# Block-sparse attention with a mixture of experts: gathered v rows interleaved by slot, edge blocks joined with a running maximum, masks made later

## The chip, the cores and the metric

One core of a Trainium2 chip runs the program. The metric is the device time of one execution in microseconds (us), as a median of several runs. The engines are PE (matrix products; its weight loads are listed as PEld), DVE (vector), ACT (scalar and table functions), POOL (general, and the issuer of gathers by index) and SP (issuer of most DMA transfers). PSUM is the memory that PE writes to, SBUF the one that it reads from.

## The reference

There are 4 batches of 8 heads, 768 positions and head dimension 64. Positions form 24 blocks of 32. A query block sees its own block and both neighbours, the first and the last block, and three blocks that the input `sampled_blocks` names for it; the first and the last query block see everything.

```python
scores = scale * np.matmul(q, k.transpose(0, 1, 3, 2))
mask = np.abs(blk_i - blk_j) <= window
mask = mask | (blk_i == 0) | (blk_j == 0) | (blk_i == n_blocks - 1) | (blk_j == n_blocks - 1)
for qb in range(n_blocks):
    for kb in sampled_blocks[qb]:
        mask[qb * block:(qb + 1) * block, kb * block:(kb + 1) * block] = True
scores = np.where(mask, scores, -1000000000.0)
attn = np.exp(scores - np.max(scores, axis=-1, keepdims=True))
attn = attn / (np.sum(attn, axis=-1, keepdims=True) + 1e-09)
attn_out = np.matmul(attn, v)
...
for e in range(E):
    h = np.maximum(x @ w1[e], 0.0)
    out += p[:, e:e + 1] * (h @ w2[e])
```

`x` is the attention output with a token's 512 numbers in a row, 3072 tokens in all. There are 4 experts with 1024 hidden numbers.

## The kernel before

The order of all instructions on all engines is the order of the program's text. Attention works in units, 16 a batch. Each unit has four steps: S (scores, maximum, exponential), T (PE transposes the probabilities), A (the product with v) and X (PE transposes the result into `xr`, the input of the experts).

The first four units of a batch are of the class `Edge`. They treat the first and the last query block (`i` = 0, 1) against all keys, in two halves of 384 keys (`m` = 0, 1). The maximum of each half is kept in `mx`, its sum in `sums`, and the product of the first half in `eo`. A of the second half joins both: it forms the common maximum `top`, the two weights `ew` (DVE, then an exponential on ACT, then DVE again), and the weighted and normalised sum `xe`, which X transposes into `xt`.

The other twelve are of the class `Group`. A unit treats four query blocks and half of the heads. A query row has 8 slots of 32 keys: the window's three blocks, the first block, three sampled blocks, the last block. In S, PE writes scores of two heads into each of two PSUM tiles `s`; DVE adds the mask `mk` and takes the maximum in one instruction (L321, whose result goes to the SBUF tile `p`), and ACT takes the exponential in place (L324). In T, four transposes of 128 columns go into `tp`, and ACT or DVE copies them to `pt`. So after the transpose the partition of a key is its slot in a half of four, times 32, plus its row in the block. v must lie in SBUF in that same order: `v[:, i, 0]` has the window and the first block, `v[:, i, 1]` the sampled blocks and the last one.

`load_v0` (batch 0) and `load_v` (later) bring v: one SP transfer for the window's 96 rows of two query blocks, one for the first block's 32, and a gather by POOL for each query block with the row numbers `vidx`. In batch 0 six tiles are used in turn; the last block's rows are put there once for each, by SP, and the gathers bring 96 rows. The row numbers come from `row_numbers`: two small matmuls, `rows` and `floor`, turn the sampled block numbers into rows. `spread_mask` makes the mask of all groups: a reduction and a product on DVE, a matmul `mps` and a copy to `mask`. `sampled_block` reads a block number into a register of ACT or POOL, and `copy_k` copies the sampled key blocks into `kr` with it. Both `rows`, `floor`, `mps` and the transposes `tw` and `tp` of batch 0 take turns in the PSUM pool `a`, which has two buffers.

Batch 0's attention runs alone, about 100 us. Its loop takes n from 0 to 18 and issues S of unit n, X of n - 3, A of n - 2 and T of n - 1, with loads and weight preparation between. Then the experts of batch b - 1 run with the attention of batch b between their pieces; `drive` interleaves them by planned times. There the transposes share the two PSUM buffers of `s`, and ACT copies both halves of T. The experts' additions on DVE (L810, L843, L942 and others) empty PSUM tiles that PE then fills again; L698 and L932 are the experts' matmuls.

Of the kernel before, what the change touches and what calls it, by code (L numbers as in the profile page):

```python
# [8 lines left out]
F32 = mybir.dt.float32  # L9
# [14 lines left out]
def attention_moe_kernel(ctx: ExitStack, tc, qb, kb, vr, sampled, sampled_t, probs, w1, w2, out):  # L24
# [122 lines left out]
    def load_v0(t, c):  # L147

        js = blocks(t)[c:c + 2]
        if not js:  # L150
            return
        turn = vturn[0]
        vturn[0] += 1
        if turn < 6:
            vtiles.append(pool["v"].tile([P, 2, 2, DM], F32, name=f"v{turn}"))
        v = vtiles[turn % 6]
        rows = vr[(js[0] - 1) * BLOCK:(js[0] + 2) * BLOCK]
        nc.sync.dma_start(v[:3 * BLOCK, :len(js), 0],
                          bass.AP(rows.tensor, rows.offset,
                                  [[DM, 3 * BLOCK], [BLOCK * DM, len(js)], [1, DM]]))  # L160
        if turn < 6:
            nc.sync.dma_start(v[3 * BLOCK:, :, 0],
                              vr[:BLOCK].unsqueeze(1).broadcast_to([BLOCK, 2, DM]))
            nc.sync.dma_start(v[3 * BLOCK:, :, 1],
                              vr[S - BLOCK:S].unsqueeze(1).broadcast_to([BLOCK, 2, DM]))
        for i, j in enumerate(js):
            nc.gpsimd.indirect_dma_start(
                out=v[:3 * BLOCK, i, 1], out_offset=None, in_=vr, element_offset=0,
                in_offset=bass.IndirectOffsetOnAxis(ap=vidx[:3 * BLOCK, j:j + 1], axis=0))
            gathered[0, t][2][c + i] = v[:, i]  # L170

    def load_v(b, t, cs=range(QG)):
        js = blocks(t)
        for c in range(min(cs), min(max(cs) + 1, len(js)), 2):
            n = min(2, len(js) - c)
            v = pool["v"].tile([P, 2, 2, DM], F32, name="v")
            rows = vr[b * S + (js[c] - 1) * BLOCK:b * S + (js[c] + 2) * BLOCK]
            nc.sync.dma_start(v[:3 * BLOCK, :n, 0],
                              bass.AP(rows.tensor, rows.offset,
                                      [[DM, 3 * BLOCK], [BLOCK * DM, n], [1, DM]]))  # L180
            nc.sync.dma_start(v[3 * BLOCK:, :n, 0],
                              vr[b * S:b * S + BLOCK].unsqueeze(1).broadcast_to([BLOCK, n, DM]))
            for i in range(n):
                nc.gpsimd.indirect_dma_start(  # L184
                    out=v[:, i, 1], out_offset=None, in_=vr, element_offset=b * S * DM,
                    in_offset=bass.IndirectOffsetOnAxis(ap=vidx[:, js[c + i]:js[c + i] + 1], axis=0))
                gathered[b, t][2][c + i] = v[:, i]

# [13 lines left out]
    for c in range(QG):  # L202
        sampled_block(1 + c, 1)
# [3 lines left out]
    nc.gpsimd.affine_select(out=lead, in_=lead, pattern=[[1, P]], compare_op=ALU.is_ge,  # L207
                            fill=0.0, base=0, channel_multiplier=-BLOCK)
    nc.gpsimd.affine_select(out=lead, in_=lead, pattern=[[-1, P]], compare_op=ALU.is_ge,
                            fill=0.0, base=BLOCK - 1, channel_multiplier=BLOCK)  # L210
# [29 lines left out]
    def row_numbers():  # L240
# [7 lines left out]
        nc.vector.tensor_sub(within, within, floor_[:, :1])  # L248
# [18 lines left out]

    def spread_mask():
        ind4 = p1.tile([NB, P], F32, name="ind4")
        nc.vector.reduce_sum(ind4, ind.rearrange("n t p -> n p t"), axis=AX.X)  # L270
        nc.vector.tensor_mul(sel, sel, bad.unsqueeze(1).broadcast_to([NB, NG, SLOTS]))
        mps = pool["a"].tile([P, NG, SLOTS], F32, name="mps", tag="a")
        nc.tensor.matmul(mps.rearrange("p t n -> p (t n)"), ind4, sel.rearrange("p t n -> p (t n)"),
                         start=True, stop=True)
        nc.vector.tensor_copy(mask, mps)
# [13 lines left out]
    class Group:  # L289
# [4 lines left out]
        def S(self):  # L294
# [21 lines left out]
            for i in range(HH):  # L316
                for h in range(2):
                    m = 2 * i + h
                    mx = at.tile([P, 1], F32, name="mx", bufs=4)
                    p = self.p[:n, m]  # L320
                    nc.vector.tensor_tensor_reduce(p.rearrange("p (a b) -> p a b", b=BLOCK),  # L321
                                                   s[h][:n, i], mk, -SCALE, 3.0e38, ALU.add, ALU.min,
                                                   mx[:n])
                    nc.scalar.activation(p, p, AF.Exp, bias=mx[:n], scale=-1.0,  # L324
                                         accum_out=self.sums[:n, m:m + 1])
# [43 lines left out]
    class Edge:  # L369
# [4 lines left out]
        def S(self):  # L374
# [10 lines left out]
            if m == 0:  # L385
                edge["S"] = [at.tile([P, 2, 2], F32, name=f"edge{j}") for j in range(2)]
            self.mx, self.sums = edge["S"]
            self.p = pool["p"].tile([P, S], F32, name="pw", tag="p")
            nm = at.tile([P, 2], F32, name="nm2")
            for h in range(2):  # L390
                nc.vector.reduce_max(self.mx[:, m, h:h + 1], s[h], axis=AX.X)
            nc.vector.tensor_scalar(nm, self.mx[:, m], -SCALE, None, op0=ALU.mult)
            for h in range(2):
                nc.scalar.activation(self.p[:, h * HS:(h + 1) * HS], s[h], AF.Exp, bias=nm[:, h:h + 1],
                                     scale=SCALE, accum_out=self.sums[:, m, h:h + 1])

# [9 lines left out]
        def A(self):  # L406
# [10 lines left out]
            if self.m == 0:  # L417
# [3 lines left out]
            top = at.tile([P, 2], F32, name="top")  # L421
            nc.vector.tensor_max(top, self.mx[:, 0], self.mx[:, 1])
            w = at.tile([P, 2, 2], F32, name="ew")
            nc.vector.tensor_sub(w, self.mx, top.unsqueeze(1).broadcast_to([P, 2, 2]))
            nc.scalar.activation(w, w, AF.Exp, scale=SCALE)
            nc.vector.tensor_mul(self.sums, self.sums, w)
            rec = at.tile([P, 2], F32, name="rec2")
            nc.vector.scalar_tensor_tensor(rec, self.sums[:, 0], 1e-9, self.sums[:, 1],
                                           op0=ALU.add, op1=ALU.add)
            nc.vector.reciprocal(rec, rec)  # L430
            nc.vector.tensor_mul(w, w, rec.unsqueeze(1).broadcast_to([P, 2, 2]))
            self.xg = at.tile([P, P], F32, name="xe", bufs=1)
            xe = self.xg.rearrange("p (h d) -> p h d", d=D)
            eo = edge["o"]
            nc.vector.tensor_mul(xe, eo, w[:, 0].unsqueeze(2).broadcast_to([P, 2, D]))
            nc.vector.tensor_mul(eo, o, w[:, 1].unsqueeze(2).broadcast_to([P, 2, D]))
            nc.vector.tensor_add(xe, xe, eo)
# [648 lines left out]
    with ExitStack() as only:  # L1086
# [11 lines left out]
        rows = {0: (0, 2), 1: (1, 0), 2: (1, 2), 5: (2, 0), 6: (2, 2)}  # L1098
        rows.update({2 * t + 1: (t, 0) for t in range(3, NG)})
        rows.update({2 * t + 2: (t, 2) for t in range(3, NG)})  # L1100
# [4 lines left out]
        for n in range(N + 3):  # L1105
            if n < N:
                us[n].S()
            if n == 0:
                row_numbers()
                load_v0(0, 0)  # L1110
            if n == 1:
                spread_mask()
                copy_k(0, 0)
# [7 lines left out]
            if n in rows:  # L1121
                t, c = rows[n]
                if c == 0:
# [12 lines left out]
            if n < 4:  # L1136
                for c in range(QG + 5 * n, min(QG + 5 * n + 5, NB - 2)):
# [127 lines left out]
```

## Time and profile before

| | us |
|---|---|
| median of 3 runs | 1277.0 |
| lowest and highest | 1276.53, 1279.74 |
| the profiled execution, whole | 1275.48 |
| its span, from the first to the last instruction | 1273.5 |
| PE busy | 1207.7 |
| DVE busy | 847.6 |
| POOL busy | 840.4 |
| ACT busy | 520.3 |

The mean granted clock of PE is 0.983 of full speed. The span is what the trace covers; the 2.0 us around it are start and end. A view's row has a start or a count, a duration, the engine, the line of the kernel (L321 is line 321), the operation with output and input, and in brackets the idle time of that engine just before, with what ended it. Busy time of an engine that nobody waits for costs nothing; what counts is idle time of PE, which is nearly full, and what it waits for.

### The profile page before, as it was taken

The numbers are of one execution on the slowest core, as the hardware profiler recorded it, in microseconds if no ns is written. First come the engines' busy times: TensorE is split into PE (matmuls) and PEld (weight loads), VectorE is DVE, ScalarE is ACT, GpSimd is POOL, SyncE is SP. The second block draws the span as 40 slices with busy tenths as digits, with TensorE's granted clock in tenths as the row PEclk, the third lists the DMA queues.
The fourth block names the chain that finished last, engine by engine and source line by source line (L and its number), as shares of the span: only waits on it lengthen the run. The fifth ranks groups of instructions, "written<-read, shape, count | busy, mean of one in ns | idle before, by whom it ended". The sixth has DMA issues, their size and how long they took to land.

```text
span 1273.5 us, 32610 instructions
## 1 busy us (share of the span) xinstructions
PE 1207.7 (95%) x12583; PEld 1111.6 (87%) x12583; DVE 847.6 (67%) x1710; ACT 520.3 (41%) x1259; POOL 840.4 (66%) x788
## 2 busy tenths in 40 slices
PE   6778899999999899999999989999999999999997
PEld 3667778888888888999999978998999999999997
DVE  5565577676765566766676875766676776666667
ACT  3473545656454244444442343444443323222221
POOL 6353778888867475765746774676754777666663
PEclk8899999999999999999999999999999999999999
DMA  9675588989877866899868875998886777887774
GB/s 290 168 238 177 184 321 276 346 290 341 312 286 290 302 215 210 271 271 294 263 218 302 257 253 170 286 269 254 272 261 215 235 250 251 260 267 248 250 243 149
DMA packets 212822, 326.52 MB, mean 256 GB/s; under 512 B 15995, under 2 KB 115932, under 8 KB 212668
## 3 DMA queue, kind: packets, MB, share of 16 engines
q1 hardware_dynamic: 205936, 302.80, 73.8%
q0 software_dynamic: 6688, 21.63, 5.6%
q8 instruction: 100, 1.64, 0.5%
q14 instruction: 54, 0.44, 0.1%
q10 hardware_dynamic: 44, 0.00, 0.0%
HBM read 256.69 MB, written 67.68 MB: 255 GB/s over the span
## 4 chain that ended last, share of the span: by engine, by line
PE 63%; DVE 4%; DMA 3%; issue 1%; ACT 1%; POOL 0%; SPq 0%; DVEq 0%; ACTq 0%
PE w L698 16%; PE u L932 15%; PE v L698 12%; PE v L932 11%; PE o L346 2%; PE tp L333 2%; DMA wo<-kept 2%; PE po L768 1%; PE s L311 1%; PE s L306 1%; DVE ha L810 1%; DVE tot L942 1%; DMA v<-in_vr_dram,vidx 1%; DVE xo L475 0%; DMA k<-in_kb_dram 0%
## 5 line engine op out<-in xcount | busy, mean ns | idle before, releaser
L856 POOL TENSOR_TENSOR ho<-ha,ho 128x768 fp32r<-128x768 f32 x165 | 324.2, 1974 | 233.4 <-ACT ho L855 219.4
L698 PE MATMUL w<-xo,wo 128*128 128x384 f32 x1536 | 315.6, 342 | 18.8 <-DVE ha L843 11.4
L698 PEld LDWEIGHTS w<-xo,wo 128*128 128x128 f32 x1536 | 271.6, 190 | 30.6 <-DVE ha L843 14.0
L698 PE MATMUL v<-xo,wo 128*128 128x384 f32 x1200 | 244.9, 340 | 5.4 <-DVE hl L717 1.5
L855 ACT CAST ho<-ha 128x768 fp32r<-128x768 f32 x168 | 139.5, 836 | 266.9 <-DVE ha L810 95.6
L932 PE MATMUL u<-ho,w2o 128*128 128x384 f32 x1128 | 229.5, 339 | 0.4 <-issue 0.4
L698 PEld LDWEIGHTS v<-xo,wo 128*128 128x128 f32 x1200 | 212.5, 189 | 12.5 <-DVE hl L717 2.1
L932 PEld LDWEIGHTS u<-ho,w2o 128*128 128x128 f32 x1128 | 198.9, 189 | 2.6 <-issue 2.0
L932 PE MATMUL v<-ho,w2o 128*128 128x384 f32 x888 | 181.2, 341 | 2.5 <-issue 1.5
L932 PEld LDWEIGHTS v<-ho,w2o 128*128 128x128 f32 x888 | 156.6, 190 | 4.7 <-issue 2.2
L942 DVE TENSOR_TENSOR tot<-v,tot 128x384 f32<-128x384 f32 x184 | 97.7, 550 | 62.6 <-PE v L932 60.2
L942 DVE TENSOR_TENSOR tot<-u,tot 128x384 f32<-128x384 f32 x180 | 99.0, 553 | 54.1 <-PE u L932 52.4
L324 ACT ACTIVATE p<-p,mx 128x256 f32<-128x256 f32 (+1 forms) x192 | 95.4, 498 | 89.5 <-DVE mx L321 89.3
L810 DVE SCALAR_TENSOR_TENSOR ha<-ha,pb 128x384 f32<-128x384 f32 x126 | 127.4, 1011 | 4.4
L768 PE MATMUL po<-w2o,hh 128*128 128x512 f32 x384 | 123.2, 402 | 5.3 <-DVE oacc L783 3.5
L588 POOL TENSOR_TENSOR wo<-r,wo 128x256 fp32r<-128x256 f32 x92 | 73.9, 810 | 44.7 <-ACT wo L587 44.6
L321 DVE CUSTOM_DVE_ANT_1 p<-s,mask 128x256 f32<-128x256 f32 (+1 forms) x192 | 69.7, 417 | 29.0 <-PE s L311 28.7
L184 POOL DMA_INDIRECT v<-in_vr_dram,vidx x66 | 65.3, 989 | 29.9 <-issue 13.5
L768 PEld LDWEIGHTS po<-w2o,hh 128*128 128x128 f32 x384 | 68.7, 188 | 15.5 <-DVE oacc L783 4.8
L768 PE MATMUL po<-w2o,hl 128*128 128x512 f32 x192 | 75.7, 394 | 0.0
L346 PEld LDWEIGHTS o<-v,pt 128*32 128x32 f32 x2816 | 47.8, 112 | 18.7 <-issue 14.9
L346 PE MATMUL o<-v,pt 128*32 128x64 f32 x2816 | 57.5, 225 | 5.5 <-issue 4.2
(162 smaller groups left out, 1642.5 us busy)
## 6 DMA issues: line engine op xcount, KB each, us to landing
w2o<-kept SPq DMA_DIRECT2D x168, 512.0 KB
wo<-kept SPq DMA_DIRECT2D x318, 256.0 KB
kept<-wo SPq DMA_DIRECT2D x106, 256.0 KB
v<-in_vr_dram SPq DMA_DIRECT2D x44, 384.0 KB
kept<-w2o SPq DMA_DIRECT2D x32, 512.0 KB
r<-in_w_dram SPq DMA_DIRECT2D x16, 512.0 KB
r<-in_w_dram SPq DMA_DIRECT2D x32, 256.0 KB
kept<-t SPq DMA_DIRECT2D x32, 256.0 KB
```

The lines of the kernel that those rows point to most:

```text
L184: nc.gpsimd.indirect_dma_start(out=v[:, i, 1], out_offset=None, in_=vr, element_offset=b * S * DM, in_offset=bass.IndirectOffsetOnAxis(ap= ...
L321: nc.vector.tensor_tensor_reduce(p.rearrange("p (a b) -> p a b", b=BLOCK), s[h][:n, i], mk, -SCALE, 3.0e38, ALU.add, ALU.min, mx[:n])
L324: nc.scalar.activation(p, p, AF.Exp, bias=mx[:n], scale=-1.0, accum_out=self.sums[:n, m:m + 1])
L346: nc.tensor.matmul(o[cs, m], self.pt[:, 2 * m + k, cs], vs[c][:, k, e], start=k == 0, stop=k == 1)
L588: nc.gpsimd.tensor_sub(o[:, 1], src, f32(o[:, 0]))
L698: nc.tensor.matmul(ps, w[:, wi, t], x[:, xi, t], start=fresh and m == 0, stop=m == 3 * KH - 1, skip_group_check=not fresh)
L768: nc.tensor.matmul(p, a[:, js], w[:, i], start=f == 0 and n == 0, stop=f == FT - 1 and n == 2)
L810: nc.vector.scalar_tensor_tensor(block(g, half), src, 0.0, q, op0=ALU.max, op1=ALU.mult)
L855: nc.scalar.copy(o[:, 0], src)
L856: eng.tensor_sub(o[:, 1], src, f32(o[:, 0]))
L932: nc.tensor.matmul(ps, w[:, j, wi, ds], h[:, hi, j], start=fresh and m == 0, stop=m == 5, skip_group_check=not fresh)
L942: nc.vector.tensor_add(t, ps, t)
```

## The change

Four things are changed.

1. v lies in SBUF with a key's partition at 4 x row + slot. The window's load becomes three SP transfers of 32 rows, each to every fourth partition; the first block's goes to every fourth one from 3. All gathers bring 128 rows, in batch 0 too, where the six separate transfers of the last block go. The matrix `lead` and the arithmetic behind `vidx` follow.
2. The probabilities take the same order: DVE writes the masked scores back into the PSUM tile `s`, and ACT reads them there and writes the exponentials to `p` in steps of four elements.
3. In an `Edge` unit the second half takes its maximum over both halves in S, and the weight of the first half is made there, with an exponential on ACT behind the scores' own. A scales the first half's sum and product by it, adds, and normalises.
4. In batch 0, `row_numbers` and the DVE part of `spread_mask` move from units 0 and 1 behind T of unit 0, the mask's matmul and `copy_k` behind T of unit 1. ACT reads eight block numbers ahead of the loop instead of four.

```diff
+    def window(v, b, js):
+        for m in range(3):
+            rows = vr[b * S + (js[0] + m - 1) * BLOCK:]
+            nc.sync.dma_start(v[m:P:QG, :len(js), 0],
+                              bass.AP(rows.tensor, rows.offset,
+                                      [[DM, BLOCK], [BLOCK * DM, len(js)], [1, DM]]))
+
+    def first_rows(v, b, n):
+        nc.sync.dma_start(v[3:P:QG, :n, 0],
+                          vr[b * S:b * S + BLOCK].unsqueeze(1).broadcast_to([BLOCK, n, DM]))
+
+    def gather(v, b, i, j):
+        nc.gpsimd.indirect_dma_start(
+            out=v[:, i, 1], out_offset=None, in_=vr, element_offset=b * S * DM,
+            in_offset=bass.IndirectOffsetOnAxis(ap=vidx[:, j:j + 1], axis=0))
...
-    for c in range(QG):
+    for c in range(2 * QG):
         sampled_block(1 + c, 1)
...
-        nc.vector.tensor_sub(within, within, floor_[:, :1])
+        nc.vector.scalar_tensor_tensor(within, floor_[:, :1], -1.0 / BLOCK, within,
+                                       op0=ALU.mult, op1=ALU.add)
+        nc.vector.tensor_scalar(within, within, 1.0 / QG, None, op0=ALU.mult)
...
-                    p = self.p[:n, m]
-                    nc.vector.tensor_tensor_reduce(p.rearrange("p (a b) -> p a b", b=BLOCK),
-                                                   s[h][:n, i], mk, -SCALE, 3.0e38, ALU.add, ALU.min,
-                                                   mx[:n])
-                    nc.scalar.activation(p, p, AF.Exp, bias=mx[:n], scale=-1.0,
-                                         accum_out=self.sums[:n, m:m + 1])
+                    p = self.p[:n, m].rearrange("p (a r b) -> p a b r", a=2, b=QG)
+                    sc = s[h][:n, i]
+                    nc.vector.tensor_tensor_reduce(sc, sc, mk, -SCALE, 3.0e38, ALU.add, ALU.min, mx[:n])
+                    nc.scalar.activation(p, sc.rearrange("p (a b) r -> p a b r", b=QG), AF.Exp,
+                                         bias=mx[:n], scale=-1.0, accum_out=self.sums[:n, m:m + 1])
...
+            if m == 1:
+                nc.vector.tensor_max(self.mx[:, 1], self.mx[:, 0], self.mx[:, 1])
             nc.vector.tensor_scalar(nm, self.mx[:, m], -SCALE, None, op0=ALU.mult)
+            if m == 1:
+                nc.vector.tensor_sub(self.w, self.mx[:, 0], self.mx[:, 1])
...
+            if m == 1:
+                nc.scalar.activation(self.w, self.w, AF.Exp, scale=SCALE)
...
-            if n == 0:
-                row_numbers()
-                load_v0(0, 0)
-            if n == 1:
-                spread_mask()
-                copy_k(0, 0)
...
+            if n == 1:
+                row_numbers()
+                spread_mask()
+            if n == 2:
+                place_mask()
+                copy_k(0, 0)
```

The order of the instructions shows three places. The first is the start of PE's program before, and then after; `sw` are scores of an Edge unit, `tw` its transposes, `ow` its products with v.

```order
L198 MATMUL idle<-zero 128x384 x4
L382 MATMUL sw<-k,qe 32x384 x8
L245 MATMUL rows<-slot,lead 128x24
L247 MATMUL floor<-quad,lead 128x128
L382 MATMUL sw<-k,qe 32x384 x8
L273 MATMUL mps<-sel,ind_312 128x48
L403 MATMUL tw<-ident,pw 128x128 x6
L382 MATMUL sw<-k,qe 32x384 x8
L415 MATMUL ow<-vn,ptw 32x64 x24
```

Here is the same place in the changed kernel.

```order
L199 MATMUL idle<-zero 128x384 x4
L387 MATMUL sw<-k,qe 32x384 x16
L416 MATMUL tw<-ident,pw 128x128 x6
L246 MATMUL rows<-slot,lead 128x24
L248 MATMUL floor<-quad,lead 128x128
L387 MATMUL sw<-k,qe 32x384 x8
L428 MATMUL ow<-vn,ptw 32x64 x24
L416 MATMUL tw<-ident,pw 128x128 x6
L279 MATMUL mps<-sel,ind_225 128x48
```

The scores of two units and the transposes of the first now come ahead of `rows`, and `mps` stands behind the second unit's transposes. The second place is DVE's program at the first join, before, with the semaphores that each row waits for:

```order
30 L391 TENSOR_REDUCE edge_484<-sw 128x1 [waits PE_49] x2
31 L392 TENSOR_SCALAR nm_593<-edge_484 128x2 [waits DVE_49,Activation_49]
32 L422 TENSOR_TENSOR top<-edge_221 128x2
33 L424 TENSOR_TENSOR ew<-edge_221,top 128x4 [waits DVE_49]
34 L426 TENSOR_TENSOR edge_222<-edge_222,ew 128x4 [waits Activation_49]
35 L428 SCALAR_TENSOR_TENSOR rec_630<-edge_222 128x2 [waits DVE_49]
36 L430 RECIPROCAL rec_630<-rec_630 128x2 [waits DVE_49]
37 L431 TENSOR_TENSOR ew<-ew,rec_630 128x4 [waits DVE_49]
38 L435 TENSOR_TENSOR xe<-eo,ew 128x128 [waits DVE_49]
39 L436 TENSOR_TENSOR eo<-ow,ew 128x128 [waits DVE_49,PE_49]
40 L437 TENSOR_TENSOR xe<-xe,eo 128x128 [waits DVE_49]
```

and after:

```order
33 L398 TENSOR_REDUCE edge_379<-sw 128x1 [waits PE_49] x2
34 L400 TENSOR_TENSOR edge_379<-edge_379 128x2 [waits DVE_49]
35 L401 TENSOR_SCALAR nm_587<-edge_379 128x2 [waits DVE_49,Activation_49]
36 L403 TENSOR_TENSOR ew<-edge_379 128x2
37 L435 TENSOR_TENSOR rec_621<-edge_259,ew 128x2 [waits Activation_49]
38 L436 SCALAR_TENSOR_TENSOR rec_621<-rec_621,edge_259 128x2 [waits DVE_49]
39 L437 RECIPROCAL rec_621<-rec_621 128x2 [waits DVE_49]
40 L440 SCALAR_TENSOR_TENSOR eo<-eo,ew,ow 128x64 [waits PE_49]
41 L440 SCALAR_TENSOR_TENSOR eo<-eo,ew,ow 128x64
42 L443 TENSOR_TENSOR xe<-eo,rec_621 128x128 [waits DVE_49]
```

The maximum and the weight stand with the scores, and the join waits for ACT on its first row alone, for a result that a row of an earlier step asked for. The third place is DVE's program in a Group unit (the second one of the batch, whose four reductions are of two PSUM tiles in turn), after:

```order
55 L328 ISA s,mx<-s,mask 128x256 [waits PE_49]
56 L328 ISA mx 128x1
57 L328 ISA s,mx<-s,mask 128x256 [waits PE_49]
58 L328 ISA mx 128x1
59 L328 ISA s,mx<-s,mask 128x256 [waits Activation_49]
60 L328 ISA mx 128x1
61 L328 ISA s,mx<-s,mask 128x256 [waits Activation_49]
62 L328 ISA mx 128x1
```

The third and the fourth wait for ACT, which is the first and the second exponential of the same unit. Before, they were `p,mx<-s,mask`, and what waits for ACT they had was for exponentials of the unit ahead.

More of the change, by code (lines that the diff above doesn't have):

```diff
@@ L176, in load_v @@
             v = pool["v"].tile([P, 2, 2, DM], F32, name="v")
[L177 to L182, printed above, removed]
+            window(v, b, js[c:c + n])
+            first_rows(v, b, n)
             for i in range(n):
-                nc.gpsimd.indirect_dma_start(
-                    out=v[:, i, 1], out_offset=None, in_=vr, element_offset=b * S * DM,
-                    in_offset=bass.IndirectOffsetOnAxis(ap=vidx[:, js[c + i]:js[c + i] + 1], axis=0))
+                gather(v, b, i, js[c + i])
                 gathered[b, t][2][c + i] = v[:, i]
@@ L386, in S @@
                 edge["S"] = [at.tile([P, 2, 2], F32, name=f"edge{j}") for j in range(2)]
+                edge["w"] = at.tile([P, 2], F32, name="ew")
             self.mx, self.sums = edge["S"]
+            self.w = edge["w"]
             self.p = pool["p"].tile([P, S], F32, name="pw", tag="p")
@@ L420, in A @@
                 return
[L421 to L426, printed above, removed]
             rec = at.tile([P, 2], F32, name="rec2")
-            nc.vector.scalar_tensor_tensor(rec, self.sums[:, 0], 1e-9, self.sums[:, 1],
-                                           op0=ALU.add, op1=ALU.add)
+            nc.vector.tensor_mul(rec, self.sums[:, 0], self.w)
+            nc.vector.scalar_tensor_tensor(rec, rec, 1e-9, self.sums[:, 1], op0=ALU.add, op1=ALU.add)
             nc.vector.reciprocal(rec, rec)
-            nc.vector.tensor_mul(w, w, rec.unsqueeze(1).broadcast_to([P, 2, 2]))
+            eo = edge["o"]
+            for h in range(2):
+                nc.vector.scalar_tensor_tensor(eo[:, h], eo[:, h], self.w[:, h:h + 1], o[:, h],
+                                               op0=ALU.mult, op1=ALU.add)
             self.xg = at.tile([P, P], F32, name="xe", bufs=1)
[L433 to L437, printed above, removed]
+            nc.vector.tensor_mul(self.xg.rearrange("p (h d) -> p h d", d=D), eo,
+                                 rec.unsqueeze(2).broadcast_to([P, 2, D]))
         def X(self):
@@ L1120, in attention_moe_kernel @@
                 us[n - 1].T(1)
-            if n in rows:
-                t, c = rows[n]
-                if c == 0:
+            if n == 1:
[4 more added lines that the diff above has]
+                copy_k(0, 0)
+            for t, c in rows.get(n, ()):
+                if c == 0 and t:
                     load_q(0, t)
@@ L1135, in attention_moe_kernel @@
                 taken += 1
-            if n < 4:
-                for c in range(QG + 5 * n, min(QG + 5 * n + 5, NB - 2)):
+            if 0 < n < 4:
+                for c in range(5 * n + 3, min(5 * n + 8, NB - 2)):
                     sampled_block(1 + c, 1)
```

31 lines of the change are left out of this document (12 added, 19 removed).

## The prediction

> **What bounds the kernel now.** I read the page first, for the engine that is full and for the one group of matmuls that still waits.
>
> ```profile
> span 1273.5 us, 32610 instructions
> PE 1207.7 (95%) x12583; PEld 1111.6 (87%) x12583; DVE 847.6 (67%) x1710; ACT 520.3 (41%) x1259; POOL 840.4 (66%) x788
> ...
> L698 PE MATMUL w<-xo,wo 128*128 128x384 f32 x1536 | 315.6, 342 | 18.8 <-DVE ha L843 11.4
> ```
>
> PE is busy for 95% of the span, so only its 65.8 idle us are to be had. The table by stage says where they lie.
>
> ```profile
> 0.00:31.00 31.00, 19.34 (x306) 0.87 0.97 287
> 41.00:100.00 59.00, 46.18 (x1271) 0.90 0.68 207
> 100.00:1273.00 1173.00, 1134.34 (x10759) 0.99 0.80 258
> ```
>
> Columns: length, PE busy, granted clock, DMA share, GB/s. PE idles 11.7 us in the first 31, 12.8 in the rest of batch 0's attention from 41 on, and 38.7 in the 1173 us behind. Two of PE's waits before 100 us that name no other engine matter below:
>
> ```profile
> PE s L306 <- issue: 6.1, 9, 2.6
> PE ow L415 <- issue: 2.8, 3, 1.2
> ```
>
> Columns: total, times, longest. "issue" is time for which the profile shows no wait. The waits that the change touches stand in PE's timeline (start, length, what it is, idle time before):
>
> ```profile
> 8.68 0.37 PE L245 MATMUL rows<-slot,lead 4*128 4x24 f32 x2 [1.53 <-DVE slot L243]
> 13.56 0.63 PE L273 MATMUL mps<-sel,ind 24*128 24x48 f32 x2 [3.40 <-DVE sel L271]
> 14.12 1.54 PE L403 MATMUL tw<-ident,pw 128*128 128x128 f32 x6
> 15.59 0.89 PE L382 MATMUL sw<-k,qe 64*32 64x384 f32 x8
> 19.65 0.88 PE L382 MATMUL sw<-k,qe 64*32 64x384 f32 x16
> 25.57 0.40 PE L306 MATMUL s<-k,q 64*32 64x96 f32 x16
> 29.23 0.33 PE L442 MATMUL xt<-ident,xe 128*128 128x128 f32 x1 [2.44 <-DVE xe L435]
> 35.59 0.40 PE L306 MATMUL s<-k,q 64*32 64x96 f32 x16
> 39.15 0.33 PE L442 MATMUL xt<-ident,xe 128*128 128x128 f32 x1 [2.16 <-DMA v<-in_vr_dram]
> ```
>
> The four idle times are rows, mps and, twice, xt. I call the units 0, 1, 2 ... in their order: S(0) is the first scores, T the transposes, A the product with v.
>
> **The start, step by step.** The mask leaves the path at 13.56, and two things take its place: ACT reads eight block numbers instead of four ahead of its first exponential, and the rows matmul stands behind T(0), in a PSUM buffer that ACT's copy of T(0) must have emptied.
>
> ```profile
> L123 ACTq TENSOR_LOAD <-sbrow x22: 275/278/478, 5.4 to 28.0; - x22
> L123 ACTq FUSED_REGOPS  x22: 147/147/167, 6.0 to 28.4; - x22
> ```
> ```profile
> 8.56 0.58 ACT L394 ACTIVATE pw<-sw,nm 128x384 f32<-128x384 f32 x1 [4.96 <-DVE slot L243]
> 15.06 0.48 ACT L404 COPY ptw<-tw 128x384 f32<-128x384 f32 x1 [1.00 <-issue]
> ...
> 36.91 0.19 ACT L425 ACTIVATE ew<-ew 128x4 f32<-128x4 f32 x1
> ```
> ```profile
> 10.73 1.02 DVE L391 TENSOR_REDUCE edge<-sw 128x1 f32<-128x384 f32 x2 [0.90 <-PE sw L382]
> ...
> 11.86 1.44 DVE L270 TENSOR_REDUCE ind<-ind 24x128 f32<-24x768 f32 x1
> ```
>
> The durations are the middle ones. A block number costs 0.278 + 0.147 us and the gaps around them, by my estimate 0.57 in all; from 5.4, eight end at about 10.0. Two exponentials take 1.2: those of S(0) then run 10.0 to 11.2, those of S(1) to 12.4, the new weight (0.2) to 12.6, the copy (0.48) to 13.1. T(0) itself can start at 11.2 instead of 14.12. rows (0.37) and the floor matmul behind it run from 13.1, and S(2) at about 13.7, 1.9 earlier than 15.59. A(0) and T(1) keep that. On DVE the row numbers come at 14.0, then the reduction (1.44), the maxima of S(2) (1.02 for two) and their scaling, and ACT's two exponentials and copy of T(1): 14.0 + 1.6 + 1.2 + 1.2 + 0.5 = 18.5 (0.2 for each small operation). The mask matmul waits for that copy, since it takes the buffer, so S(3) starts at 18.9, not 19.65: of 1.9 us, **0.75** is left. A(1), T(2) and S(4) follow with that.
>
> The first xt then waited 2.44 us for the join. In the new order the weight is ready with the scores, and behind A(1) there are two joining operations and one scaling left, some 1.1 us, while T(2) and S(4) take longer on PE. I count all **2.4**. So 3.2 us by 29.23, if POOL keeps up:
>
> ```profile
> 10.12 1.10 POOL L167 DMA_INDIRECT v<-in_vr_dram,vidx  x1 [4.15 <-DVE vidx L249]
> 17.71 0.52 POOL L141 COPY kr<-k 128x128 f32 x2
> 25.84 0.52 POOL L141 COPY kr<-k 128x128 f32 x2
> ```
>
> Its gathers start at 14.1, 4.0 later, so its key copies end at 22.2 and 30.4, against S(4) at 24.8 and S(6) at 32.4 in the new order. Both are in time, the second by 2.0 us.
>
> **The join.** In the second one DVE goes through nine operations and a trip to ACT:
>
> ```profile
> 35.84 0.16 DVE L422 TENSOR_TENSOR top<-edge 128x2 f32<-128x2 f32 x1
> ...
> 37.14 0.16 DVE L426 TENSOR_TENSOR edge<-edge,ew 128x4 f32<-128x4 f32 x1 [0.94 <-ACT ew L425]
> ...
> 38.32 0.29 DVE L436 TENSOR_TENSOR eo<-ow,ew 128x128 f32<-128x128 f32 x1
> 38.65 0.45 DVE L437 TENSOR_TENSOR xe<-xe,eo 128x128 f32<-128x128 f32 x1
> ```
>
> That is 3.26 us, and xt starts 0.05 after its end: the wait was for DVE, whatever the wait's label says. New: three small operations at 0.2, two joining ones at about 0.3, one scaling at 0.3 to 0.45: 1.6 us. That saves **1.7** of the 2.16. In the later batches six joins run beside the MoE; one is paid in full by PE:
>
> ```profile
> 761.67 0.16 DVE L426 TENSOR_TENSOR edge<-edge,ew 128x4 f32<-128x4 f32 x1 [1.22 <-ACT ew L425]
> 762.47 1.92 DVE L435 TENSOR_TENSOR xe<-eo,ew 128x128 f32<-128x128 f32 x1
> 766.10 2.29 PE L698 MATMUL w<-xo,wo 128*128 128x384 f32 x6 [5.41 <-DVE ha L843]
> ```
>
> The trip of 1.22 goes, and one large operation less; one that is stretched to 1.92 can stay. I count **2.0** here, between 1.2 and 3.5, and nothing for the other five, whose matmuls share what is left of the 11.4 us of L698.
>
> **Probabilities in slot order.** DVE now writes the masked scores back to PSUM and ACT reads them there. Two heads share a PSUM tile, so the third reduction of a unit waits for the unit's own first exponential.
>
> ```profile
> 35.15 0.42 DVE L321 CUSTOM_DVE_ANT_1 p<-s,mask 128x256 f32<-128x256 f32 x1
> 35.50 0.42 DVE L321 CUSTOM_DVE_ANT_1 p<-s,mask 128x256 f32<-128x256 f32 x1
> ```
> ```profile
> 34.93 0.51 ACT L324 ACTIVATE p<-p,mx 128x256 f32<-128x256 f32 x1 [2.48 <-DVE mx L321]
> 35.44 0.49 ACT L324 ACTIVATE p<-p,mx 128x256 f32<-128x256 f32 x1
> ```
>
> DVE's four go at 0.35 each, 1.46 with the last; now the third can start only behind the first exponential, 0.5 + 0.5 us after the first reduction, the fourth 0.5 after that, and the last ends at about 1.95: +0.5 us on DVE, nothing on ACT, whose four are as dense as before. Queued behind on DVE are the unit's normalisation, pt copies, and in later batches the MoE additions that PE waits for: 36 units, 18 us of DVE, where PE idles 38.7 of 1173, so DVE's own reserve covers most of it; I charge about a twelfth, **+1.5**, with 0 and 18 as the ends. In batch 0 the waits with a cause above are at the start, so 0.
>
> ACT's writes are now 16 bytes apart. No row shows that. Between L394 (0.58 for 384 elements) and L324 (0.49 for 256) an element costs 0.7 ns, 256 of them 0.18 us: the ends are 0 and, if each cost double, 0.18 us an instruction. I take 0, since the rows show ACT's fixed part to be the larger. [...] No row of before shows such a write.
>
> **Loads of v.** 44 window loads become 132, each a third of the size. A direct load takes SP 0.32 us to issue (estimate from the row below), so 88 more are 28 us of SP over the span, behind which weight refills queue; I charge 0, with +3 as the end. The first loads' rate:
>
> ```profile
> 759.67 0.32 SPq L602 DMA_DIRECT2D wo<-kept  x1
> ```
> ```profile
> GB/s 0 31 172 406 338 445 377 408 403 391 383 350 234 238 236 256 244 295 285 297 272 268 240 238 260 254 295 299 305 295 397 369 287 176 39 193 145 285 223 186
> ```
>
> One number is 1 us. Loads of 128 partitions run at about 390 until 11 us, those of 96 and 32 partitions at 234 to 305 behind. PE waits for none of them by the list, so the forecast has 0.
>
> **The sum.** 0.75 + 2.4 + 1.7 + 2.0 - 1.5 = 5.4 us off. The profiled execution took 1275.5 us (span 1273.5), and the median of the runs is 1277.0: 1270.1 by the one, **1271.6** by the other, which I forecast.
>
> **Rivals.** A change of up to 0.3% (3.8 us) can't be told from none here.
>
> *The start gives nothing back* (20%). S(3) is held by ACT's copy, or S(6) by POOL, 2.0 us in hand; later joins stay hidden. Then 1.7 is gained and 1.5 lost: 1276.5.
>
> *More from the ports* (17%). The 2.8 us of "issue" before the ow matmuls and the longest before s, 2.6, may come from a full DMA. If they do, spread loads end them: at 390 instead of 265 GB/s the 18 us of v loads take 12. 5.4 us more, 1266. [...]
>
> *DVE held by ACT* (15%). If six tenths of the 18 us reach PE, the gains are used up: 18 x 0.6 = 10.8 against 6.9 gained gives 1281. It decides where an addition that PE waits for follows a unit's last reduction within 0.5 us. Against it: DVE is at 67%. For it: the 11.4 us of L698 show that PE has no reserve where DVE comes late, and ACT may itself be at a 0.8 us cast when the exponential is due.
>
> The gain above has 48%. Of it I give 0.41 to more than 0.3% (below 1273.2), 0.07 to less. Faster is 0.41 + 0.17 = 0.58, same 0.07 + 0.20 = 0.27, slower 0.15. The range leaves out the slow tail above 1279 and the fast one below 1264.5; the forecast's own is 1268 to 1275.
>
> **What would show it.** Right: no mps wait near 13 us, first scores of a Group near 24.8, xt without idle time twice, third reductions 0.5 us after the second, the exponential near 0.5 us. Wrong: PE waiting for ACT's copy before S(3) past 19.7; S(6) waiting for kr; L698's wait for L843 above 11.4; an exponential above 0.65 us with PE waiting for pt; "issue" before 50 us at a few tenths.

## The result, and the profile after

The changed kernel took 1270.1 us (median of 8 runs, 1267.3 to 1271.2) against 1276.9 us (8 runs, 1272.3 to 1280.7) for the kernel before: a ratio of 0.9943, 95% interval 0.9924 to 0.9963. It is faster by 7 us, between 5 and 10. The prediction said 1271.6, and faster. Its sum came out for the wrong reasons, as the parts below show: the join alone gives far more, and the other two parts cost.

The profiled execution took 1267.3 us. These rows are its page's span and engines, and the two groups of instructions whose form changed (busy time, mean ns, idle time before).

```profile
span 1265.6 us, 32714 instructions
PE 1203.7 (95%) x12583; PEld 1102.7 (87%) x12583; DVE 862.1 (68%) x1703; ACT 540.2 (43%) x1259; POOL 838.3 (66%) x788
...
L705 PE MATMUL w<-xo,wo 128*128 128x384 f32 x1536 | 313.9, 341 | 17.4 <-DVE ha L850 9.8
...
L329 ACT ACTIVATE p<-s,mx 128x256 f32<-128x256 f32 (+1 forms) x192 | 123.9, 720 | 80.2 <-DVE mx L328 80.0
...
L328 DVE CUSTOM_DVE_ANT_1 s<-s,mask 128x256 f32<-128x256 f32 (+1 forms) x192 | 80.3, 438 | 51.6 <-PE s L317 24.2 <-ACT p L329 22.5 <-issue 0.9
```

The same two groups before:

```profile
L324 ACT ACTIVATE p<-p,mx 128x256 f32<-128x256 f32 (+1 forms) x192 | 95.4, 498 | 89.5 <-DVE mx L321 89.3
...
L321 DVE CUSTOM_DVE_ANT_1 p<-s,mask 128x256 f32<-128x256 f32 (+1 forms) x192 | 69.7, 417 | 29.0 <-PE s L311 28.7
```

The exponential went from 498 to 720 ns. The reduction waits 22.5 us in all for ACT, 0.47 for each of 48 units: that wait is as long as was worked out. The table by stage follows (length, PE busy, and near the end the granted clock).

```profile
0.00:31.00 31.00, 20.76 (x192) 11.25 (x192) 15.52 (x46) 8.28 (x27) 19.13 (x49) 0.75 0.86 301
41.00:100.00 59.00, 46.04 (x1387) 35.28 (x1372) 40.94 (x145) 41.73 (x123) 30.29 (x49) 1.00 0.75 242
100.00:1265.00 1165.00, 1128.25 (x10751) 1050.05 (x10749) 800.39 (x1491) 483.94 (x1090) 785.10 (x683) 1.00 0.79 260
```

Next is the start in PE's timeline (start, length, what it is, idle time before). The line numbers are those of the changed kernel.

```profile
11.23 1.02 PE L416 MATMUL tw<-ident,pw 128*128 128x128 f32 x6 [2.84 <-ACT pw L405]
13.07 0.59 PE L246 MATMUL rows<-slot,lead 4*128 4x24 f32 x2 [0.81 <-DVE slot L244]
...
14.19 1.53 PE L387 MATMUL sw<-k,qe 64*32 64x384 f32 x16
15.65 1.26 PE L428 MATMUL ow<-vn,ptw 128*32 128x64 f32 x30
17.23 0.40 PE L428 MATMUL ow<-vn,ptw 128*32 128x64 f32 x2 [0.32 <-issue]
...
20.96 0.50 PE L428 MATMUL ow<-vn,ptw 128*32 128x64 f32 x8 [0.46 <-issue]
...
22.87 0.66 PE L279 MATMUL mps<-sel,ind 24*128 24x48 f32 x2
23.45 1.53 PE L387 MATMUL sw<-k,qe 64*32 64x384 f32 x16
...
31.33 0.57 PE L312 MATMUL s<-k,q 64*32 64x96 f32 x16
...
35.01 0.33 PE L449 MATMUL xt<-ident,xe 128*128 128x128 f32 x1
...
40.57 0.40 PE L312 MATMUL s<-k,q 64*32 64x96 f32 x16
...
44.58 0.33 PE L449 MATMUL xt<-ident,xe 128*128 128x128 f32 x1
```

T(0) starts at 11.23 (11.2 was worked out), rows at 13.07 (13.1), S(2) at 14.19 (13.7). Both xt rows have no idle time before them. But from 17 us on the matmuls of A(0) come in small groups with "issue" between, and S(3), due at 18.9, starts at 23.45; S(4), due at 24.8, starts at 31.33, and S(6), due at 32.4, at 40.57, five microseconds later than before. Then the one wait that had been seen to be paid in full:

```profile
758.12 1.31 PE L705 MATMUL w<-xo,wo 128*128 128x384 f32 x6 [1.65 <-DVE ha L850]
```

It was 5.41 us, and it is now 1.65.

To see where the time comes from, I compare the start times of the same expert matmul, by its number, in profiled executions. The differences to before, in us, are taken at seven of them; the first row has the time in the kernel before. The runs of these names are described below; two of the kernels have a second profiled execution, in the third session.

```
                     first   225    319    439    522    789   1003
changed               -2.2  -5.1   -1.5   -1.3   -4.8   -9.9   -6.0
changed (third)       -0.7  -4.0   -0.6   -0.3   -3.9   -8.6   -4.9
join alone            -3.1  -7.0   -6.5   -6.9   -9.8  -15.3  -11.2
join (third)          -2.6  -6.3   -6.5   -4.5   -8.1  -15.0  -10.9
start alone           -1.0  +0.1   +0.2   +0.4   +1.1   +1.3   +1.3
order alone           -2.2  -2.1   +1.3   +0.8   +3.2   +4.4   +7.9
```

"First" stands at 100 us, the first expert matmul. Two executions of one kernel differ by up to 2.4 us here, so smaller differences say nothing. The changed kernel gains in steps, ahead of 225, 522 and 789, where each later batch's edge units are, and gives time back behind each step, where the Group units are. The step ahead of 789 is partly given back in every kernel that has the join, so the column of 1003 counts for what is kept.

### The profile page after: what moved, and what is told of

Read it like the earlier page. It is cut to its first block, busy times and chain, and to the rows that moved or that the text cites. A ratio compares the mean times of both kernels' runs of the same rounds, so it can differ in the third digit from the quotient of the medians.

```text
span 1265.6 us, 32714 instructions
## 1 busy us (share of the span) xinstructions
PE 1203.7 (95%) x12583; PEld 1102.7 (87%) x12583; DVE 862.1 (68%) x1703; ACT 540.2 (43%) x1259; POOL 838.3 (66%) x788
## 4 chain that ended last, share of the span: by engine, by line
PE 60%; DVE 6%; DMA 2%; POOL 2%; ACT 2%; issue 1%; SPq 0%; DVEq 0%; ACTq 0%; POOLq 0%
PE w L705 16%; PE u L939 14%; PE v L705 12%; PE v L939 11%; PE o L351 2%; PE tp L338 2%; DVE ha L817 1%; PE po L775 1%; PE s L317 1%; DMA wo<-kept 1%; PE s L312 1%; DVE tot L949 1%; POOL ho L863 1%; ACT p L329 1%; DVE xo L482 1%
## 5 line engine op out<-in xcount | busy, mean ns | idle before, releaser
L705 PEld LDWEIGHTS w<-xo,wo 128*128 128x128 f32 x1536 | 268.9, 189 | 31.4 <-DVE ha L850 13.5
L329 ACT ACTIVATE p<-s,mx 128x256 f32<-128x256 f32 (+1 forms) x192 | 123.9, 720 | 80.2 <-DVE mx L328 80.0
L817 DVE SCALAR_TENSOR_TENSOR ha<-ha,pb 128x384 f32<-128x384 f32 x126 | 130.6, 1037 | 4.4
L176 POOL DMA_INDIRECT v<-in_vr_dram,vidx x88 | 86.0, 978 | 53.7 <-PE o L351 20.1
L328 DVE CUSTOM_DVE_ANT_1 s<-s,mask 128x256 f32<-128x256 f32 (+1 forms) x192 | 80.3, 438 | 51.6 <-PE s L317 24.2
L351 PEld LDWEIGHTS o<-v,pt 128*32 128x32 f32 x2816 | 46.5, 110 | 18.9 <-issue 15.6
```

Source lines behind the costliest of these rows:

```text
L176: nc.gpsimd.indirect_dma_start(out=v[:, i, 1], out_offset=None, in_=vr, element_offset=b * S * DM, in_offset=bass.IndirectOffsetOnAxis(ap= ...
L328: nc.vector.tensor_tensor_reduce(sc, sc, mk, -SCALE, 3.0e38, ALU.add, ALU.min, mx[:n])
L329: nc.scalar.activation(p, sc.rearrange("p (a b) r -> p a b r", b=QG), AF.Exp, bias=mx[:n], scale=-1.0, accum_out=self.sums[:n, m:m + 1])
L351: nc.tensor.matmul(o[cs, m], self.pt[:, 2 * m + k, cs], vs[c][:, k, e], start=k == 0, stop=k == 1)
L705: nc.tensor.matmul(ps, w[:, wi, t], x[:, xi, t], start=fresh and m == 0, stop=m == 3 * KH - 1, skip_group_check=not fresh)
L817: nc.vector.scalar_tensor_tensor(block(g, half), src, 0.0, q, op0=ALU.max, op1=ALU.mult)
```

## The experiments

All of these were timed in rounds with the kernel before on the same chip. The kernel before took 1276.1, 1270.4 and 1275.7 us in three sets of runs, each on one chip and called sessions below, so medians are compared within a session.

**First session: each part alone.** `e1_join_only` takes from the diff only what touches the class Edge:

```diff
+            if m == 1:
+                nc.vector.tensor_max(self.mx[:, 1], self.mx[:, 0], self.mx[:, 1])
...
+            if m == 1:
+                nc.scalar.activation(self.w, self.w, AF.Exp, scale=SCALE)
...
-            nc.scalar.activation(w, w, AF.Exp, scale=SCALE)
...
+                nc.vector.scalar_tensor_tensor(eo[:, h], eo[:, h], self.w[:, h:h + 1], o[:, h],
+                                               op0=ALU.mult, op1=ALU.add)
```

> The kernel before with the new edge join alone. If the join carries the gain: 4 to 6 us less than before (ratio 0.995 to 0.997), xt without idle time in batch 0, and the wait of the expert matmul near 766 us down from 5.4 to about 1.7 us. If the gain is the order of v or the start: 2 us less at most (ratio above 0.998).

It took 1262.4 us, a ratio of 0.9886 (0.9867 to 0.9905): two to three times what was expected, and faster than the whole change.

`e2_start_only` takes the moves in batch 0's loop and the eight block numbers:

```diff
-    for c in range(QG):
+    for c in range(2 * QG):
...
-            if n == 0:
-                row_numbers()
...
+            if n == 1:
+                row_numbers()
+                spread_mask()
+            if n == 2:
+                place_mask()
```

> The kernel before with the later masks and the eight block numbers alone. If the start gives what the prediction counted: 0.75 us or more off (ratio 0.9985 to 0.9995), S(3) near 18.9. If the later row numbers cost as much as the mask gives, as the start of the changed kernel suggests (S(6) at 40.6 there against 35.6 before): 0 to 4 us more (ratio 1.000 to 1.003).

1279.5 us, 1.0030 (1.0013 to 1.0047): it costs, as the second reading said. Its profiled execution was the fastest of its twelve runs and has the span of the kernel before, 1273.5 us, so the row "start alone" above can't show where the cost lies.

`e3_order_only` takes the loads of v, `lead` and `within`, and the probabilities:

```diff
+        window(v, 0, js)
...
+                    p = self.p[:n, m].rearrange("p (a r b) -> p a b r", a=2, b=QG)
...
+                    nc.vector.tensor_tensor_reduce(sc, sc, mk, -SCALE, 3.0e38, ALU.add, ALU.min, mx[:n])
```

> The kernel before with the new order of v and of the probabilities alone. If DVE's wait for ACT and the slower exponentials (720 ns against 498) are covered and the loads were not waited for: within 1.5 us of before (ratio 0.999 to 1.001). If spread loads carry the gain: 3 us or more off (below 0.998). If the serial reductions cost what was charged: 1.5 us more or worse (above 1.001).

1280.7 us, 1.0030 (1.0015 to 1.0044): it costs too. That spread loads carry the gain is refuted. The three parts add up to -1.14% + 0.30% + 0.30% = -0.54%, and the whole change has -0.57%.

`e7_late_v` asks for the first gathered v rows one unit later:

```diff
-        rows = {1: [(0, 0), (0, 2)], 2: [(1, 0)], 3: [(1, 2)], 5: [(2, 0)], 6: [(2, 2)]}
+        rows = {2: [(0, 0), (0, 2)], 3: [(1, 0)], 4: [(1, 2)], 5: [(2, 0)], 6: [(2, 2)]}
```

> The changed kernel with the first four loads of gathered v asked for one unit later, behind the key copies. If the idle times called issue before the ow matmuls come from DMA queues full of v: A(0) and A(1) take about 1.5 us each instead of 5.7 and 5.0, S(4) starts at 26 or earlier instead of 31.3, and the kernel is 3 to 5 us faster than the changed one (ratio to before about 0.991). If they come with the place in the program, whatever the DMA does: A(0) stays above 4 us and the time at the changed kernel's (0.994).

1271.3 us, 0.9953 (0.9932 to 0.9974), as the changed kernel's 0.9943. In PE's timeline A(0) takes 1.51 us in one piece, as the first reading said, but the idle time only moved. PE's rows, and one of ACT:

```profile
16.53 1.51 PE L428 MATMUL ow<-vn,ptw 128*32 128x64 f32 x48
17.96 1.02 PE L416 MATMUL tw<-ident,pw 128*128 128x128 f32 x6
23.24 0.66 PE L279 MATMUL mps<-sel,ind 24*128 24x48 f32 x2 [4.26 <-issue]
```
```profile
22.71 0.48 ACT L417 COPY ptw<-tw 128x384 f32<-128x384 f32 x1 [2.70 <-remote]
```

4.26 us of idle time now stand in one place before mps. They are labelled "issue", but mps takes the PSUM buffer that this copy empties, and starts 0.05 us after the copy's end: PE waited for ACT. ACT in turn was idle for 2.70 us, though the transposes that it copies were done at 18.98; what held it the profile does not show. Neither reading holds: the idle time is not tied to A(0), and moving these loads does not end it.

**Second session: what in each part does it.** `e6_in_place_only` is the kernel before with the scores written back to PSUM, in the old order:

```diff
-                                                   s[h][:n, i], mk, -SCALE, 3.0e38, ALU.add, ALU.min,
...
+                    nc.vector.tensor_tensor_reduce(sc, sc, mk, -SCALE, 3.0e38, ALU.add, ALU.min, mx[:n])
+                    nc.scalar.activation(p.rearrange("p (a b) -> p a b", b=BLOCK), sc, AF.Exp, bias=mx[:n], scale=-1.0,
```

> The kernel before with the masked scores written back to PSUM and the exponential reading them there, in the old order with writes in a row. If DVE's wait for ACT is what the new order costs: 2.5 us or more over before (ratio 1.002 or above). If it is ACT's write in steps of 16 bytes, or the loads: within 1.5 us (ratio 0.999 to 1.001), and the exponential near 500 ns instead of 720.

1275.0 against 1270.4 us, 1.0029 (1.0010 to 1.0048). So by the medians the writing back alone costs as much as the whole new order, within intervals that are wide; a stretch of the trace, further below, says less. Its two groups in the list by line:

```profile
L323 ACT ACTIVATE p<-s,mx 128x256 f32<-128x256 f32 (+1 forms) x192 | 89.1, 468 | 96.5 <-DVE mx L322 91.3
...
L322 DVE CUSTOM_DVE_ANT_1 s<-s,mask 128x256 f32<-128x256 f32 (+1 forms) x192 | 80.2, 438 | 43.7 <-PE s L311 28.6 <-ACT p L323 14.9
```

Reading PSUM and writing in a row took 468 ns here; so of the changed kernel's 720 ns the writes in steps of 16 bytes are 252, about 1.0 ns for each of 256 elements.

`e8_reductions_first` has order and join, with the four reductions ahead of the four exponentials:

```diff
+            for m in range(2 * HH):
+                mx = at.tile([P, 1], F32, name="mx", bufs=4)
+                mxs.append(mx)
+                sc = s[m % 2][:n, m // 2]
+                nc.vector.tensor_tensor_reduce(sc, sc, mk, -SCALE, 3.0e38, ALU.add, ALU.min, mx[:n])
+            for m in range(2 * HH):
...
+                nc.scalar.activation(p, sc.rearrange("p (a b) r -> p a b r", b=QG), AF.Exp,
```

> The new order and the new join without the new start; in a Group unit all four reductions are issued ahead of the four exponentials, so that DVE never waits for its own unit's exponential. The two parts alone add up to a ratio of 0.9886 + 0.0030 = 0.9916. If DVE's wait is what the order costs: 0.989 or below. If the slower exponential is: 0.9916 or above, since ACT now starts later too.

1262.9 us, 0.9939 (0.9918 to 0.9960). Against the sum of the first session that reads as no help, but the kernel before was 5.7 us faster in the second one, and order with join was not run beside it. By the time this one is inconclusive; the same stretch further below tells more.

`e9_mask_later` has the join, and of the start only the mask's part:

```diff
-                spread_mask()
                 copy_k(0, 0)
...
+            if n == 1:
+                spread_mask()
+            if n == 2:
+                place_mask()
```

> The new join, and of the new start only the later mask (its DVE part behind T(0), its matmul behind T(1)); the row numbers, the four block numbers and the key copies stay where they were. The join alone has 0.9886. If the mask held the start and the late row numbers gave it back: 0.9865 or below, T(0) near 11 and S(3) near 18. If the mask's wait is only passed on: 0.988 to 0.990.

1261.0 us, 0.9914 (0.9890 to 0.9937), the fastest of the session. T(0) starts at 10.10 and S(3) at 17.93, as expected; the ratio is in neither of the two ranges, and can't be held against the first session's.

`e10_no_round_trip` makes the weight early, as the new join does, and keeps the two products and the sum. The edit is shown against the join alone:

```diff
-                nc.vector.scalar_tensor_tensor(eo[:, h], eo[:, h], self.w[:, h:h + 1], o[:, h],
-                                               op0=ALU.mult, op1=ALU.add)
...
+            nc.vector.tensor_mul(xe, eo, w.unsqueeze(2).broadcast_to([P, 2, D]))
+            nc.vector.tensor_mul(eo, o, rec.unsqueeze(2).broadcast_to([P, 2, D]))
+            nc.vector.tensor_add(xe, xe, eo)
```

> The weight of the first half is made in S as in the new join, but the products are taken apart as before: two products and a sum where the new join has two joining operations and a scaling. If the round trip to ACT in the middle of DVE's program is what cost the time: two thirds of the join's 14.5 us or more (ratio 0.992 or below). If the number of operations on two SBUF inputs beside POOL is: less than a third (above 0.996).

1262.8 us, 0.9932 (0.9908 to 0.9956), 1.8 us behind e9_mask_later, which has the later mask as well. That misses the 0.992 of the first reading, though the interval holds it, and is clearly below the 0.996 of the second. By the same last matmul its profiled execution is 10.7 us ahead of before, the join's 13.4; by the ratios it has 0.68% where the join alone has 1.14% and, in the third session, 0.83%. So more than half of the gain, 0.6 to 0.8 of it, is in making the weight early, and with it the round trip; that the fewer operations are the rest is likely, but no run beside it on the same chip shows it.

**Third session: the parts on one chip.** The edits are those of e1_join_only (join), the whole diff (changed), the diff without the start (join and order), and e9_mask_later (mask).

> The new join alone once more, beside the three below, since the kernel before took 1276.1 us in one session and 1270.4 in another. If the parts add up: the fastest of these with, or near, the later mask; 6 us or more below the whole change. If the join's 14.5 us belonged to that session's kernel before: within 3 us of the whole change.

1265.1 us (1262.4 to 1266.8), 0.9917 (0.9886 to 0.9948).

> The whole change. If the join gains and the other two parts cost 0.3% each: 6 to 9 us above the join alone.

1269.9 us (1266.0 to 1273.9), 0.9960 (0.9937 to 0.9982).

> The new join and the new order, with the start as before. If order and start each cost 0.3%: midway, 3 to 5 us above the join alone and 3 to 5 below the whole change. If the start is the whole cost: as the join alone. If the order is: as the whole change.

1267.0 us (1260.2 to 1268.5), 0.9927 (0.9899 to 0.9955).

> The new join with the later mask alone, the row numbers early. If the mask's wait at the start was worth something: 1.5 us or more below the join alone. If the start is set by the idle times called issue and the low clock there, whatever waits for what: within 1.5 us of the join alone.

1261.7 us (1258.6 to 1263.3), 0.9886 (0.9855 to 0.9917).

So on one chip: join 1265.1, with the order 1267.0, with the start too 1269.9. The steps are 1.9 (which is within the noise) and 2.9 us, somewhat less than the 0.3% (3.8 us) each that the parts alone had; the whole change is 4.8 us above the join, less than the 6 that was expected. The later mask by itself takes 3.4 us off the join where the whole new start adds 2.9 to join and order, so what costs in the start is likely the rest of it: the late row numbers and key copies, or the eight block numbers. The intervals of these ratios overlap, and the profiled executions of join and join with mask took 1262.4 and 1262.0 us, so the traces can't show the 3.4. Join and later mask together beat both kernels, with no run of it as slow as the fastest run of the whole change.

## Why the prediction was right, and where its steps were wrong

**The first step, 0.75 us by S(3), failed.** The waits were worked out rightly up to S(2), but S(3) came at 23.45 and not at 18.9: A(0), which took 1.51 us before, ran from 15.65 to 21.46, with "issue" between its matmuls. To see how much of the removed waits came back under that name, I add up PE's waits in the first 95 us from the rows of each kernel. The label has to be checked first. In the join alone, third session, mps is put down to "issue", and it starts 0.14 us after `sel` is ready, as it did before (0.15 us, with the label `sel`):

```profile
14.72 0.28 DVE L271 TENSOR_TENSOR sel<-sel,bad 24x48 f32<-24x48 f32 x1
```
```profile
15.14 0.63 PE L273 MATMUL mps<-sel,ind 24*128 24x48 f32 x2 [4.10 <-issue]
```

So idle times that end within 0.15 us of the instruction on which the matmul depends are counted with the others here: 1.2 us of the kernel before, 4.1 of each join alone, 4.3 of the later v, 0.6 of the second execution of the changed kernel.

```
                        issue   all others    sum
before                   13.1         12.2   25.3
changed                  15.7          7.1   22.8
changed (third session)  15.3          5.9   21.2
start alone              15.2          7.6   22.8
order alone              12.5         11.5   24.0
join alone               16.2          7.4   23.6
join (third session)     15.7          7.6   23.3
join with later mask     18.1          7.1   25.2
v later                  12.1         11.9   24.0
```

In the changed kernel the other waits fall by 5.1 us and "issue" grows by 2.6, in its second execution by 6.3 and 2.2. So a third to a half of what was removed came back under that name, with the join and the later mask nearly all. The sum is little else than 95 us less the time in which PE is busy (69.6 before, 71.9 and 73.7 in the two executions of the changed kernel, at clocks of 0.87, 0.91 and 0.86), so a sum that stays does not show that waits were passed on. Behind "issue" the profile shows no wait; what it is was not tested, and why it grows stays open.

The rival that had the loads of v behind these gaps has two runs against it. e7_late_v moved loads and gaps and gained nothing. And in e3_order_only, which has the start of before, the loads of v did speed up. These are its rates per us:

```profile
GB/s 0 31 148 418 341 436 391 410 401 387 385 381 391 412 371 373 404 377 381 379 275 311 379 404 408 408 293 49 0 238 164 139 8 16 0 168 203 227 227 272
```

From 12 to 19 us they are 371 to 412, where the kernel before had 234 to 297 in the same stretch, so the prediction's estimate of 390 for spread loads held here. What sets the rate, by the rival's name the ports, no run shows. Yet "issue" was 12.5 us against 13.1, and the kernel was slower. Under the new start the same loads gain less, as the changed kernel's rates show:

```profile
GB/s 0 43 129 393 377 425 395 412 393 391 391 383 381 373 277 234 281 234 293 279 303 272 324 336 307 375 406 358 254 205 119 0 16 94 176 242 21 16 0 156
```

From 14 to 23 us they run at 234 to 336. Gathers by POOL run in the same stretch, as they do from 11 us on in e3_order_only; why the rate is lower here was not found.

**2.4 and 1.7 us for the two xt waits: the waits went, the time did not all stay.** By the first expert matmul the changed kernel was 2.2 us ahead, not 4.9, in its second execution 0.7, and the join alone 3.1. The start's own cost is in that too. And the 2.2 can't be put down to the removed waits: at S(6) the kernel was 5.0 us behind, and it caught up between 41 and 100 us, where its granted clock was 1.00 against 0.90 before. How much of that is the clock's, no run separates.

**2.0 us for the later batches, with nothing for the other five joins, was the large miss.** It is the term that was mis-sized. The join alone gained 8 us behind the first expert matmul (3.1 there, 11.2 at 1003). Of these, 6.7 come by 522, from joins for which the prediction had nothing. The first join of the second batch shows how, in DVE's timeline of the kernel before:

```profile
162.13 0.15 DVE L422 TENSOR_TENSOR top<-edge 128x2 f32<-128x2 f32 x1
...
163.67 0.49 DVE L426 TENSOR_TENSOR edge<-edge,ew 128x4 f32<-128x4 f32 x1 [0.76 <-ACT ew L425]
...
166.42 0.29 DVE L437 TENSOR_TENSOR xe<-xe,eo 128x128 f32<-128x128 f32 x1
166.63 0.55 DVE L749 TENSOR_TENSOR u<-w,z 128x384 f32<-128x384 f32 x1
```

The chain holds DVE for 4.5 us, from 162.13 to 166.63, and an expert's addition (u, L749) stands right behind it. PE waited for that addition, and in the third batch for one more:

```profile
167.23 1.31 PE L698 MATMUL w<-xo,wo 128*128 128x384 f32 x6 [2.21 <-DVE u L749]
...
482.22 1.31 PE L698 MATMUL w<-xo,wo 128*128 128x384 f32 x6 [1.65 <-DVE ha L843]
```

The prediction looked for the join under L843 alone, the line that the profile's page names. The first of these waits stands under another line (u), so the group's 11.4 us did not hold it; the second stands under L843, and was left in the 11.4. With the new join, in DVE's timeline of the join alone in the third session, the same addition comes 2.1 us behind the join's start:

```profile
159.20 0.15 DVE L430 TENSOR_TENSOR rec<-edge,ew 128x2 f32<-128x2 f32 x1
...
160.58 0.77 DVE L438 TENSOR_TENSOR xe<-eo,rec 128x128 f32<-128x128 f32 x1
161.28 0.55 DVE L751 TENSOR_TENSOR u<-w,z 128x384 f32<-128x384 f32 x1
```

and PE's matmul has no idle time there. The wait at 766 fell by 3.8 us, above the upper end of 3.5, but that did not all stay: between the matmuls of 789 and 1003 the join alone loses 4.1 us again, with 5.7 us of waits for the line that was L843, where the kernel before had 3.0 (in the third session's trace).

**The charge of 1.5 us for the new order was too small.** Alone it costs 3.8 us (1.9 to 5.6). In the Group units of the second batch, one stretch with nearly the same expert matmuls, first join alone and then join with the new order (busy times of PE, PEld, DVE and on):

```profile
221.20:313.20 92.00, 91.73 (x1064) 80.35 (x1061) 59.16 (x132) 55.23 (x153) 77.71 (x103) 1.00 0.94 325
```
```profile
220.30:316.00 95.70, 92.61 (x1069) 80.46 (x1062) 64.55 (x132) 58.12 (x153) 79.23 (x104) 1.00 0.88 310
```

The stretch is 3.7 us longer. With the order, DVE is busy for 5.4 us more, and in the same window the reductions wait for ACT and PE waits for DVE:

```profile
L325 DVE CUSTOM_DVE_ANT_1 s<-s,mask 128x256 f32<-128x256 f32 x24 | 10.0, 438 | 3.8 <-ACT p L326 2.8 <-PE s L314 0.5
```
```profile
PE w L702 <- DVE z L758: 2.2, 3, 1.0
PE po L772 <- DVE oacc L787: 0.8, 1, 0.8
```

The join alone has none of these waits for ACT, and 0.3 us of PE's waits, where the order has 3.0:

```profile
L321 DVE CUSTOM_DVE_ANT_1 p<-s,mask 128x256 f32<-128x256 f32 x24 | 8.7, 416 | 0.6 <-PE s L311 0.5
```

The wait was foreseen, 0.5 us a unit; how much of it reaches PE was not. The prediction charged a twelfth of DVE's delay. With the wait (2.8 for six units) and slower reductions (10.0 against 8.7) DVE has some 0.7 us more per unit, 4.1 for six, and PE waits 2.7 us more: about two thirds. The rival in which six tenths reach PE is the one that this stretch resembles. Over the whole kernel it did not hold: 3.8 us are about two tenths of its 18.

**The exponential's writes.** The range for them was 0 to 0.18 us, and e6_in_place_only against the changed kernel gives 0.25 (720 against 468 ns): outside it. The sum had nothing for these writes. By the medians that looks right, since the in-place writing alone has the cost of the whole order. A stretch of the trace says otherwise. From the expert matmul at 225 us to the one at 319, seven profiled executions without the new order take 93.8 to 94.5 us, e6_in_place_only 94.9, and five with the whole order 97.4 to 97.6. In e6_in_place_only that window has

```profile
PE w L697 <- DVE z L753: 1.1, 3, 0.4
```
```profile
L322 DVE CUSTOM_DVE_ANT_1 s<-s,mask 128x256 f32<-128x256 f32 x24 | 10.0, 438 | 2.4 <-ACT p L323 1.8 <-PE s L311 0.5
```

With the shorter exponential the reductions wait 1.8 us for ACT, and 2.8 with the longer one. So here most of the order's cost comes with the writes in steps or with the new loads, which no run takes apart. And e8_reductions_first, where no reduction waits for an exponential, takes 99.2 us for the same stretch, of which PE waits 3.7 for one other row of DVE. That DVE's wait for ACT is what the order costs is therefore not shown.

In all: the forecast had 4.9 at the start, of which 2.2 were there at the first expert matmul, and 2.0 less 1.5 behind, where the join kept about 8 and the other parts took about 4 of it. The errors offset each other, so that the forecast came within 1.5 us of the median was luck. One of its signs of being wrong came, too: the exponential is above 0.65 us, and PE waits 0.5 us for pt in the first 95. (The first rival's 1276.5 is 1276.8 by its own terms, 1277.0 - 1.7 + 1.5.)

## What to carry to other kernels

A chain on one engine that waits in its middle for another engine can cost more than its own result. Here it held DVE for 4.5 us, and PE waited 2.21 us for the addition that stood behind it in the program's order. So look for who waits for the instructions that follow, under every line, and make the value early instead. Where idle time without a named wait fills the start of a program, don't count removed waits there as gained (here a third to a half of them came back under "issue"); and before you trust such a label, compare the start of the instruction with the end of what it depends on. When a change has several parts, time each alone: here one part was worth more than the whole.

## What was not expected of the hardware

PE's idle time for which no wait is found is 12.1 to 18.1 us in the first 95 us of the kernels of the table above, and it stands in other places in each of them. No run shows what it is.

The writes in steps of 16 bytes cost ACT about 1.0 ns for each element here (720 ns in the changed kernel against 468 in e6_in_place_only, for 256), where its whole work per element, from two lengths of the kernel before (0.58 us for 384, 0.49 for 256), is 0.7 ns.

The granted clock in the first 31 us was 0.87 in the profiled execution before and 0.75 in the one after, and 0.90 and 1.00 from 41 to 100. The start of a single profile is therefore worth little for a difference of a few microseconds.
